# Attention plus a Fourier mix on one core: a unit's maxima split and turned on VectorE instead of by a matmul with the identity

## The chip, the cores and the metric

The kernel runs on one core of one Trainium2 chip. The metric is the device time of one execution in microseconds (us); the time of a kernel is the median of its runs. Before the change it is 1856.32 us over 3 runs (1855.99 to 1856.41).

## The reference

Sequence length 2048, width 640, 32 heads of 20. Two branches are computed from the same `x` and mixed by a gate of each row:

```python
g = _sigmoid((x * gate_w).sum(-1, keepdims=True))
# branch A: softmax attention
scores = jnp.einsum("bhqd,bhkd->bhqk", q, k) * (Dh ** -0.5)
p = _softmax(scores, axis=-1)
o = jnp.einsum("bhqk,bhkd->bhqd", p, v)
a = o.transpose(...).reshape(B, S, D) @ wo
# branch B: real part of a DFT over width and sequence
y = Cr @ (x @ Wd_re.T) - Ci @ (x @ Wd_im.T)
return g * a + (1 - g) * y
```

The weights are scaled so that scores are large: the softmax needs the true maximum of each query's scores. The change concerns how that maximum gets from where it is computed to where it is subtracted.

## The kernel before, in words

Everything is float32, most of it as "float32r" parts: a number is split into a rounded part and a remainder, and products are sums of three part products. Work on TensorE is of six kinds, and the text names each by its source line:

- projections (`qk_tile`, `v_pair`, lines 119 to 121): 128 rows of the array, stationary tile of 128 columns;
- **m** matmuls (line 197): scores of 128 queries (stationary, from `q`) against 512 keys (moving, from `k`), 60 rows of the array, either rows 0 to 59 or rows 64 to 123 (one head of a pair in each half). Only their maximum over the keys is wanted: VectorE reduces each 128x512 result to a 128x1 column of the tile `mx` (line 199);
- **e** matmuls (line 949): the scores again, transposed (keys stationary, queries moving), 62 rows: 60 of `k` and `q` and 2 rows in which `k` is one and `q` holds the negated maximum in two parts, so that the maximum is subtracted in the matmul. ScalarE reads the result through the exponential (line 951);
- **F**, filler matmuls of the Fourier branch and of the output (lines 378, 635, 742): 64 rows each, issued in pairs, one for each half of the array;
- **AV** matmuls (line 556): probabilities times values, in **bursts** (all 128 rows of the array);
- one small matmul by the identity for each unit (line 231), below.

A *unit* is a pair of heads and half the queries: 32 units of 32 steps, a step being two m (or two e) matmuls. The m matmuls run 41 steps (`LEAD`) ahead of the e matmuls. The order of TensorE's work is written by hand in `ORDERS`: each cycle is a string of e, m, F and at the end B, the burst. There are three stages. From about 250 to 596 us a cycle has 8 e, 8 m, filler of the hidden DFT and a burst of 16 AV instructions. From about 600 to 1639 us a cycle has 12 e, 12 m, 48 filler matmuls of the sequence DFT and a burst of 24 AV instructions. From then to the end the filler is the output projection. Before 250 us the projections run, with the first m steps in between (`now[0] < 0` in the code).

The e and m results rotate through five PSUM banks (`bank()`), so a matmul can start only when the result five places earlier has been read.

**The turn of a unit.** At the unit's last m step the maxima of 128 queries x 8 query tiles x 2 heads stand in `mx`, a query in each partition. They are needed as rows: two single partitions of `q` for each head, 1024 queries long. Before, this takes: `max_nm` (line 213), one VectorE reduction over the four key blocks with a negation, into `nm` (128x16); `max_chain` (line 231), a TensorE matmul of `nm` with the identity into a PSUM bank of the rotation (16x128; the float32 matmul is two instructions); `split` on VectorE (lines 115 and 116), a copy to the rounded part `m1` and a subtraction to the remainder `m2`, both 16x128 and both reading that bank; and four DMAs on SP's queue (lines 239 and 240), each moving 8 partitions of 128 into one row of `q`, issued two steps later (`at_step`).

Where the turn lies is set in `burst` and in the loop at the end: if the unit's last m came before the cycle's ninth m of the second stage, `max_nm` is issued there and `max_chain` stands before the last AV step of the burst (call this *inside*); otherwise `max_nm` stands ahead of the burst and `max_chain` behind it (*behind*). In the second stage a cycle has 6 steps and a unit 32, so of three units in a row one is of the second sort. A turn comes once in about 5.3 cycles there, and once in 8 cycles of the first stage.

`dft_step` also gives VectorE an addition (line 655) at every second burst of the second stage, through `run_extras` in `burst`; `unit_end` gives it a reciprocal (line 577) for each unit.

`load_stack(0)` (line 436) loads the first `kst` and `qst` tiles by 12 DMAs from POOL's queue at about 60 us. Behind it on POOL stand the memsets of the `v` tiles (line 352), which ScalarE's evictions of the V projection (line 356) wait for.

Of the kernel before, what the change touches and what calls it, by code (L numbers as in the profile page):

```python
# [19 lines left out]
P = 128  # L20
# [9 lines left out]
KROWS = 3 * DH  # L30
NU = 2 * NP
# [41 lines left out]
def f32(ap):  # L73
    return ap.bitcast(F32)
# [3 lines left out]
def mix_kernel(ctx: ExitStack, tc: tile.TileContext, xa, wqk, wb, cdft, wo, out):  # L78
    nc = tc.nc
    pe, act, dve, pool, sp = nc.tensor, nc.scalar, nc.vector, nc.gpsimd, nc.sync  # L80
# [6 lines left out]
    small = pools(name="small", bufs=1)  # L87
# [13 lines left out]
    ident = const.tile([P, P], F32, name="ident")  # L101
# [2 lines left out]
    qst = [const.tile([P, S], R, name=f"qst{i}") for i in range(2)]  # L104
    for t in kst:
        pool.memset(f32(t), 1.0)
    logit = const.tile([P, NS], F32, name="logit")
    gate = const.tile([P, NS], F32, name="gate")
    ngate = const.tile([P, NS], F32, name="ngate")

    def split(dst1, dst2, src, e1, e2):
        if e1 is act:
            act.activation(dst1, src, AF.Copy)  # L113
        else:
            e1.tensor_copy(dst1, src)
        e2.tensor_tensor(dst2, src, f32(dst1), op=ALU.subtract)  # L116
# [11 lines left out]
    def bank():  # L128
        places.rotate(-1)
        return place_tile(places[-1])  # L130
# [49 lines left out]
    mx, nms, ends = {}, {}, []  # L180
    now, later = [-1], {}

    def at_step(i, fn):
# [3 lines left out]
    def s_mm(i, h):  # L187
        n, s = divmod(i, 32)
        if n >= NU:
            return lambda: None  # L190
        qt, kc = divmod(s, 4)
        q, k = q_unit(n), k_stack(n)
        if n not in mx:
            mx[n] = small.tile([P, 2, 8, 4], F32, name="mx", bufs=2)
        ps = bank()
        b = 64 * h
        pe.matmul(ps, q[b : b + KROWS, qt * P : (qt + 1) * P],  # L197
                  k[b : b + KROWS, kc * 512 : (kc + 1) * 512], start=True, stop=True)
        return lambda: dve.tensor_reduce(mx[n][:, h, qt, kc : kc + 1], ps, axis=AX.X, op=ALU.max)  # L199

    def s_end(i):
        n, s = divmod(i, 32)
        if n < NU and s == 31:
            if now[0] < 0:
                max_nm(n)
            else:
                ends.append(n)
        if s == 1 and 0 < n <= NU and now[0] < 0:
            max_chain(n - 1)

    def max_nm(n):
        nms[n] = small.tile([P, 16], F32, name="nm", bufs=2)
        dve.tensor_reduce(nms[n], mx.pop(n).rearrange("p h q c -> p (h q) c"), axis=AX.X, op=ALU.max, negate=True)

    def s_step(i):
        for fn in [s_mm(i, h) for h in range(2)]:
# [10 lines left out]

    def max_chain(n):
        q = q_unit(n)
        pt = bank()[:16, :P]  # L230
        pe.matmul(pt, nms.pop(n), ident, start=True, stop=True)  # L231
        m1 = small.tile([16, P], R, name="m1")
        m2 = small.tile([16, P], R, name="m2")
        split(m1, m2, pt, dve, dve)

        def rows():
            for h in range(2):
                b = 64 * h + KROWS
                sp.dma_start(f32(q[b : b + 1, :]), f32(m1[8 * h : 8 * h + 8, :]))
                sp.dma_start(f32(q[b + 1 : b + 2, :]), f32(m2[8 * h : 8 * h + 8, :]))  # L240

        if now[0] < 0:
            rows()
        else:
            at_step(now[0] + 2, rows)
# [187 lines left out]
    fin()  # L433
    flush()
    for args in load_stack(0):
        pool.dma_start(*args)
    fin = load_wqk(1)
    for s in range(12, 16, 2):
        v_pair(0, s)
# [2 lines left out]
    order = [1, ND + 1, 2, ND + 2, 3, ND + 3, 4, ND + 4]  # L442
# [16 lines left out]
    for n, c in enumerate(order):  # L459
        for t in range(4):  # L460
            m = 4 * n + t
# [362 lines left out]
    start = 4 * HID  # L824
# [152 lines left out]
    for c in range(len(goals)):  # L977
        k, base, i = phase(c)
        order, *heads_ = ORDERS[k]
        first = dict(zip("em", heads_))  # L980
        for x, kind in enumerate(order):
            if kind == "F":
                fill(c)
            elif kind == "B":
                burst(c)
            else:
                if k == 1 and kind == "m" and order[:x].count("m") == 8:
                    for n in ends:
                        max_nm(n)
                score(kind)  # L990
            if k == 1 and x == len(order) // 2:
                run_loads(c - HID)
# [114 lines left out]
```

## Time and profile before

| What | Value |
|---|---|
| Median of 3 runs | 1856.32 us |
| Span of the profiled execution, first to last instruction | 1852.1 us |
| What lies around the span (median less span) | 4.2 us |
| TensorE (PE) busy | 1844.1 us, 100% of the span |
| VectorE (DVE) busy | 1379.7 us, 74% |
| ScalarE (ACT) busy | 1357.0 us, 73% |
| GpSimd (POOL) busy | 1003.6 us, 54% |
| Granted TensorE clock, mean | 0.999 |

The profile is of one execution. In the timeline a row is a start in us from the start of the span, a duration, the engine (PE is the matmul, PEld the load of its stationary tile, SPq the DMA queue of SyncE), the source line, the operation, output and input, and a count where equal instructions have been merged; in square brackets stands the idle time before it and what ended that. In the groups by line, the columns behind the count are busy us, mean ns of one, and idle us before. A matmul's shape is written rows*columns of the array, then moving tile.

### The profile page before, as it was taken

To read this page: it belongs to the slowest core of one execution; us is meant where nothing else is said; L and a number is where in the kernel's file an instruction comes from. 1 tells how busy PE (TensorE), PEld (TensorE's weight loads), DVE (VectorE), ACT (ScalarE), POOL (GpSimd) and SP (SyncE) were. 2 spreads that over 40 slices of the span, in tenths; PEclk is the share of its full clock that TensorE was granted. 3 is DMA by queue.
4 is the path that set the end of the run, shared out by engine and by line. 5 is a ranking of instruction groups with operands and counts; after the bars stand their busy time and mean duration, and the time that the engine had idled before them with its cause. 6 is when DMAs were issued, how large, how long until landed. Compare 5 with 4: busy or idle time off the path is not lost.

```text
span 1852.1 us, 44874 instructions
## 1 busy us (share of the span) xinstructions
PE 1844.1 (100%) x17638; PEld 1365.3 (74%) x17638; DVE 1379.7 (74%) x2309; ACT 1357.0 (73%) x2645; POOL 1003.6 (54%) x832
## 2 busy tenths in 40 slices
PE   9999999999999999999999999999999999999998
PEld 8988777676776777777777777777777777776666
DVE  3044458888787888888888888888888888888853
ACT  4222258878787888888788888888888877778885
POOL 4334432121136676344677788655668767645644
PEclk9999999999999999999999999999999999999999
DMA  7744341222135574636566586646475856531233
GB/s 236 173 136 157 136 126 56 79 64 67 58 92 149 200 215 148 157 118 194 177 201 227 159 261 197 192 140 183 130 235 189 246 163 206 178 91 55 82 99 109
DMA packets 178771, 281.61 MB, mean 152 GB/s; under 512 B 44811, under 2 KB 113547, under 8 KB 178559
## 3 DMA queue, kind: packets, MB, share of 16 engines
q1 hardware_dynamic: 177599, 276.77, 49.1%
q0 software_dynamic: 960, 1.97, 0.6%
q8 instruction: 138, 2.26, 0.5%
q14 instruction: 74, 0.61, 0.1%
HBM read 214.61 MB, written 63.52 MB: 150 GB/s over the span
## 4 chain that ended last, share of the span: by engine, by line
PE 99%; DMA 0%; DVE 0%; ACT 0%; POOL 0%; SPq 0%; issue 0%; POOLq 0%; ACTq 0%
PE ps L556 25%; PE yp L635 19%; PE ps L949 17%; PE ps L197 14%; PE yp L378 7%; PE ps L119 4%; PE ps L120 4%; PE ps L121 4%; PE yp L742 3%; DMA p<-in_xa 0%; PE ps L231 0%; DVE mx L199 0%; PE ps L1041 0%; POOL x L1010 0%; PE yp L1062 0%
## 5 line engine op out<-in xcount | busy, mean ns | idle before, releaser
L199 DVE TENSOR_REDUCE mx<-ps 128x1 f32<-128x512 f32 x2048 | 1280.6, 684 | 305.8 <-PE ps L197 235.8
L951 ACT ACTIVATE p<-ps 128x512 f32<-128x512 f32 x2048 | 1055.1, 612 | 282.4 <-PE ps L197 159.3
L949 PE MATMUL ps<-qst,kst 62*128 62x512 f32 x1920 | 727.7, 406 | 0.2
L197 PE MATMUL ps<-kst,qst 60*128 60x512 f32 x1920 | 664.3, 409 | 0.0
L635 PE MATMUL yp<-x,part 64*128 64x320 f32 x5376 | 628.1, 306 | 0.0
L635 PEld LDWEIGHTS yp<-x,part 64*128 64x128 f32 x5376 | 601.7, 186 | 5.2
L556 PE MATMUL ps<-p,v 128*21 128x512 f32 (+1 forms) x4096 | 482.0, 595 | 0.0
L116 POOL TENSOR_TENSOR part<-raw,part 128x1024 fp32r<-128x1024 f32 (+1 forms) x128 | 287.4, 2246 | 338.3 <-ACT part L113 322.4
L949 PEld LDWEIGHTS ps<-qst,kst 62*128 62x128 f32 x1920 | 341.3, 185 | 155.5 <-DVE mx L199 86.4
L197 PEld LDWEIGHTS ps<-kst,qst 60*128 60x128 f32 x1920 | 323.3, 184 | 11.8 <-issue 4.2
L556 PEld LDWEIGHTS ps<-p,v 128*21 128x21 f32 (+1 forms) x4096 | 104.8, 101 | 236.1 <-issue 228.6
L378 PE MATMUL yp<-wb,x 64*128 64x320 f32 x1920 | 223.9, 307 | 0.0
L378 PEld LDWEIGHTS yp<-wb,x 64*128 64x128 f32 x1920 | 209.8, 186 | 6.5 <-ACT raw L388 0.2
L389 POOL TENSOR_TENSOR raw<-raw 128x320 f32<-128x320 f32 x64 | 55.6, 869 | 267.0 <-ACT raw L388 210.0
L515 POOL TENSOR_TENSOR raw<-raw,raw 128x1024 f32<-128x1024 f32 x77 | 187.4, 2434 | 1.5 <-DMA raw<-in_cdft 1.5
L113 ACT ACTIVATE part<-raw 128x1024 fp32r<-128x1024 f32 (+2 forms) x121 | 123.4, 1020 | 2.0 <-DMA raw<-in_wqk 1.9
L742 PE MATMUL yp<-x,part 64*128 64x320 f32 x768 | 102.2, 308 | 0.0
L116 POOL TENSOR_TENSOR x<-araw,x 128x320 fp32r<-128x320 f32 x112 | 97.4, 877 | 1.3
L338 ACT ACTIVATE p<-ps 128x512 f32<-128x512 f32 x40 | 23.7, 597 | 100.1 <-PE ps L121 97.1
L742 PEld LDWEIGHTS yp<-x,part 64*128 64x128 f32 x768 | 92.0, 186 | 1.3
L119 PE MATMUL ps<-x,part 128*128 128x512 f32 x200 | 79.9, 400 | 0.5 <-ACT x L113 0.3
L120 PE MATMUL ps<-x,part 128*128 128x512 f32 x200 | 78.6, 393 | 0.4 <-DVE x L116 0.4
(101 smaller groups left out, 1364.2 us busy)
## 6 DMA issues: line engine op xcount, KB each, us to landing
raw<-in_cdft SPq DMA_DIRECT2D x192, 512.0 KB
araw<-a_scr SPq DMA_DIRECT2D x192, 160.0 KB
qk_scr<-p SPq DMA_DIRECT2D x40, 512.0 KB
kst<-qk_scr SPq DMA_DIRECT2D x84, 160.0 KB
qst<-qk_scr SPq DMA_DIRECT2D x84, 160.0 KB
yt<-y_scr SPq DMA_DIRECT2D x80, 160.0 KB
a_scr<-raw SPq DMA_DIRECT2D x64, 160.0 KB
y_scr<-yt SPq DMA_DIRECT2D x64, 160.0 KB
```

The lines of the kernel that those rows point to most:

```text
L116: e2.tensor_tensor(dst2, src, f32(dst1), op=ALU.subtract)
L119: pe.matmul(ps, st1, mv1, start=first, stop=False)
L120: pe.matmul(ps, st1, mv2, start=False, stop=False)
L197: pe.matmul(ps, q[b : b + KROWS, qt * P : (qt + 1) * P], k[b : b + KROWS, kc * 512 : (kc + 1) * 512], start=True, stop=True)
L199: return lambda: dve.tensor_reduce(mx[n][:, h, qt, kc : kc + 1], ps, axis=AX.X, op=ALU.max)
L378: pe.matmul(yp[h][:, :HE], x[r, xz, d, cs], w[r, wz, d, :HE], start=d == 0 and z == 0, stop=d == ND - 1 and z == 2)
L515: pool.tensor_tensor(raws[0], raws[0], raws[1], op=ALU.add if PRODUCTS[n][0][1][0] > 0 else ALU.subtract)
L556: pe.matmul(t[32 * j : 32 * j + m, :], v[:, r : r + m], pp[qc][:, h, :], start=kt == 0, stop=kt == NS - 1)
L635: pe.matmul(yp[h][:, :HE], c[r, cz, cs], a[r, az], start=s == 0 and z == 0, stop=s == NS - 1 and z == 2)
L742: pe.matmul(yp[h][:, :HE], o[oz][r], wos[d, hf][r, wz], start=d == 0 and z == 0, stop=end)
L949: pe.matmul(pt, k[b : b + KROWS + 2, kt * P : (kt + 1) * P], q[b : b + KROWS + 2, qc * 512 : (qc + 1) * 512], start=True, stop=True)
L951: act.activation(pts[n, kt, qc][:, h], pt, AF.Exp, scale=float(DH) ** -0.5)
```

## The change

The line numbers of before and after differ by one or two; the diff has the code.

- `mx` is reduced over the key blocks three times in `max_chain`: the maximum (plane 1), the negated maximum written as float32r, which is its rounded part (plane 0), and the negated sum of the two, which is the remainder (plane 2). All three go to a tile `turn` (128 x 8 x 32 of float32), which is cleared once at the start of the program.
- `dve.transpose` turns each 32x32 block of `turn` into `turned` (128 x 256).
- The identity matmul, its PSUM bank, `nm`, `m1`, `m2` and the split are gone, as is the call of `max_nm` in mid-cycle. All four VectorE instructions now stand in one piece ahead of the burst's AV matmuls, behind `run_extras`.
- So that a turned row comes out in query order, the stationary tile of an m matmul is no longer 128 neighbouring queries but every eighth one: its columns lie 8 float32 (32 bytes) apart in `q`. The moving tile is unchanged.
- Each of the four row DMAs now reads 4 partitions of 256 elements.
- `load_stack(0)` goes to SP's queue, and the scratch space of software DMA is set to 4096.

```diff
+    turn = [small.tile([P, 8, 32], F32, name="turn"), small.tile([P, 256], F32, name="turned")]
+    pool.memset(turn[0], 0.0)
...
-        pe.matmul(ps, q[b : b + KROWS, qt * P : (qt + 1) * P],
+        pe.matmul(ps, q[b : b + KROWS, :].rearrange("r (c t) -> r t c", t=8)[:, qt],
                   k[b : b + KROWS, kc * 512 : (kc + 1) * 512], start=True, stop=True)
...
-    def max_nm(n):
-        nms[n] = small.tile([P, 16], F32, name="nm", bufs=2)
-        dve.tensor_reduce(nms[n], mx.pop(n).rearrange("p h q c -> p (h q) c"), axis=AX.X, op=ALU.max, negate=True)
...
     def max_chain(n):
         q = q_unit(n)
-        pt = bank()[:16, :P]
-        pe.matmul(pt, nms.pop(n), ident, start=True, stop=True)
-        m1 = small.tile([16, P], R, name="m1")
-        m2 = small.tile([16, P], R, name="m2")
-        split(m1, m2, pt, dve, dve)
+        top = mx.pop(n)
+        m = turn[0].rearrange("p t (h z c) -> p z h t c", h=2, z=4)[:, :, :, :, 0]
+        dve.tensor_reduce(m[:, 1], top, axis=AX.X, op=ALU.max)
+        dve.tensor_reduce(m[:, 0].bitcast(R), top, axis=AX.X, op=ALU.max, negate=True)
...
+            dve.tensor_reduce(m[:, 2].bitcast(R), m[:, :2].rearrange("p z h t -> p h t z"), axis=AX.X, op=ALU.add, negate=True)
+        dve.transpose(turn[1].rearrange("p (c t) -> p t c", t=8), turn[0])
...
-                sp.dma_start(f32(q[b : b + 1, :]), f32(m1[8 * h : 8 * h + 8, :]))
-                sp.dma_start(f32(q[b + 1 : b + 2, :]), f32(m2[8 * h : 8 * h + 8, :]))
+                for z in range(2):
+                    b = 64 * h + KROWS + z
+                    src = turn[1].rearrange("(b j) c -> j b c", b=4)[16 * h + 8 * z]
+                    sp.dma_start(f32(q[b : b + 1, :]), src)
...
     for args in load_stack(0):
-        pool.dma_start(*args)
+        sp.dma_start(*args)
...
     def burst(c):
-        ready = any(n in nms for n in ends)
-        for n in ends:
-            if n not in nms:
-                max_nm(n)
         k, _, i = phase(c)
         steps = 6 if k == 1 else 4
         run_extras(steps - 2)
+        while ends:
+            max_chain(ends.pop(0))
...
-            if ready and kt == (i + steps) // 2 - 1:
-                max_chain(ends.pop(0))
             av_step(now[0], kt // NS, kt % NS, kt % NS == 0 and kt > i // 2)
-        while ends:
-            max_chain(ends.pop(0))
...
-                if k == 1 and kind == "m" and order[:x].count("m") == 8:
-                    for n in ends:
-                        max_nm(n)
```

Where the instructions stand. First TensorE at a turn of the second stage that lies behind the burst (the one at 684 us in the trace), before; `ps` is a bank of the rotation, the 556 row the burst:

```order
L197 MATMUL ps_9535<-kst_86,qst_88 128x512
L197 MATMUL ps_9538<-kst_86,qst_88 128x512
L556 MATMUL ps_9058<-p,v 21x512 x12
L231 MATMUL ps_9563<-ident,nm 16x128
L949 MATMUL ps_9570<-qst_88,kst_86 128x512
L197 MATMUL ps_9574<-kst_87,qst_89 128x512
```

The same place after (m is now line 199, e 948, AV 555):

```order
L199 MATMUL ps_9502<-kst_86,qst_88 128x512
L199 MATMUL ps_9505<-kst_86,qst_88 128x512
L555 MATMUL ps_9025<-p,v 21x512 x12
L948 MATMUL ps_9533<-qst_88,kst_86 128x512
L199 MATMUL ps_9537<-kst_87,qst_89 128x512
```

The identity matmul and its bank have gone; nothing else on TensorE has moved. Now VectorE at a turn inside a burst (the one at 637 us), before; `mx` rows are reductions of m results, 655 the Fourier addition:

```order
L213 TENSOR_REDUCE nm<-mx 128x16
L199 TENSOR_REDUCE mx<-ps_8694 128x1
L199 TENSOR_REDUCE mx<-ps_8697 128x1
L199 TENSOR_REDUCE mx<-ps_8703 128x1
L199 TENSOR_REDUCE mx<-ps_8706 128x1
L655 TENSOR_TENSOR m<-yp_8427,m 128x320
L115 CAST m_8726<-ps_8724 16x128
L116 TENSOR_TENSOR m_8727<-ps_8724,m_8726 16x128
L199 TENSOR_REDUCE mx<-ps_8739 128x1
```

The same place after:

```order
L201 TENSOR_REDUCE mx<-ps_8672 128x1
L201 TENSOR_REDUCE mx<-ps_8675 128x1
L654 TENSOR_TENSOR m<-yp_8398,m 128x320
L228 TENSOR_REDUCE turn<-mx 128x2x8
L229 TENSOR_REDUCE turn<-mx 128x2x8
L231 TENSOR_REDUCE turn<-turn 128x2x8
L232 STREAM_TRANSPOSE turned<-turn 128x8x32
L201 TENSOR_REDUCE mx<-ps_8706 128x1
```

Three instructions in two places have become four in one place, behind the four reductions that are due at the burst, and behind the addition where there is one. Last, SP's queue at about 60 us, after (before, the two rows of line 435 are not there and the row of `raw<-in_wqk` follows that of `v_scr`):

```order
L329 DMA qk_scr<-p 128x2x512 x2
L329 DMA v_scr<-v 128x8x84 x2
L435 DMA kst_86<-qk_scr 20x4x512 x6
L435 DMA qst_88<-qk_scr 20x4x512 x6
L300 DMA raw<-in_wqk 128x640
L329 DMA v_scr<-v 128x8x84 x4
```

Twelve loads now stand ahead of a weight load and four stores.

More of the change, by code (lines that the diff above doesn't have):

```diff
@@ L178, in q_unit @@
         return third["q"] if p == 14 else qst[place(p)][:, u * (S // 2) : (u + 1) * (S // 2)]
-    mx, nms, ends = {}, {}, []
+    mx, ends = {}, []
     now, later = [-1], {}
@@ L204, in s_end @@
             if now[0] < 0:
-                max_nm(n)
+                max_chain(n)
             else:
                 ends.append(n)
-        if s == 1 and 0 < n <= NU and now[0] < 0:
-            max_chain(n - 1)
-    def max_nm(n):
-        nms[n] = small.tile([P, 16], F32, name="nm", bufs=2)
-        dve.tensor_reduce(nms[n], mx.pop(n).rearrange("p h q c -> p (h q) c"), axis=AX.X, op=ALU.max, negate=True)
     def s_step(i):
@@ L986, in mix_kernel @@
             else:
-                if k == 1 and kind == "m" and order[:x].count("m") == 8:
-                    for n in ends:
-                        max_nm(n)
                 score(kind)
@@ L1095 @@
     arrays = {k: c(a) for k, a in arrays.items()}
-    nc = bacc.Bacc("TRN2", target_bir_lowering=False, num_devices=1)
+    nc = bacc.Bacc("TRN2", target_bir_lowering=False, num_devices=1, dynamic_dma_scratch_size=4096)
     args = {
```

2 lines of the change are left out of this document (1 added, 1 removed).

## The prediction

> **What bounds the kernel now.** I read the page first (busy shares, the chain that ended last), then the groups of TensorE and VectorE by shape, then the timeline of TensorE around turns and around bursts without one.
>
> ```profile
> span 1852.1 us, 44874 instructions
> PE 1844.1 (100%) x17638; PEld 1365.3 (74%) x17638; DVE 1379.7 (74%) x2309; ACT 1357.0 (73%) x2645; POOL 1003.6 (54%) x832
> ...
> PE 99%; DMA 0%; DVE 0%; ACT 0%; POOL 0%; SPq 0%; issue 0%; POOLq 0%; ACTq 0%
> ...
> L199 DVE TENSOR_REDUCE mx<-ps 128x1 f32<-128x512 f32 x2048 | 1280.6, 684 | 305.8 <-PE ps L197 235.8
> ```
>
> The end is set by TensorE: it is never idle and 99% of the chain is its own work. VectorE has a quarter of the span free on the whole, 93% of its work being the reductions of m results. So two questions decide: how much of TensorE's time the turn costs, and whether the new form costs any in another place.
>
> The rhythm of the bursts answers the first. These are AV bursts (line 556) of the second and the first stage, and the identity matmuls (231) among them:
>
> ```profile
> 634.78 1.92 PE L556 MATMUL ps<-p,v 128*21 128x512 f32 x16
> 644.29 2.77 PE L556 MATMUL ps<-p,v 128*21 128x512 f32 x24
> ...
> 681.49 2.77 PE L556 MATMUL ps<-p,v 128*21 128x512 f32 x24
> 684.08 0.38 PE L231 MATMUL ps<-ident,nm 128*16 128x128 f32 x2
> 691.26 2.77 PE L556 MATMUL ps<-p,v 128*21 128x512 f32 x24
> ...
> 700.57 2.77 PE L556 MATMUL ps<-p,v 128*21 128x512 f32 x24
> 709.87 1.49 PE L556 MATMUL ps<-p,v 128*21 128x512 f32 x12
> ...
> 257.33 1.92 PE L556 MATMUL ps<-p,v 128*32 128x512 f32 x16
> ...
> 263.49 1.92 PE L556 MATMUL ps<-p,v 128*21 128x512 f32 x16
> ...
> 288.16 1.91 PE L556 MATMUL ps<-p,v 128*21 128x512 f32 x16
> ...
> 294.52 1.91 PE L556 MATMUL ps<-p,v 128*21 128x512 f32 x16
> ```
>
> Without a turn, 691.26 to 700.57 is a cycle of 9.31 us, and the next, to 709.87, is 9.30. With a turn inside the burst, 634.78 to 644.29 is 9.51: 0.20 more. With a turn behind it, 681.49 to 691.26 is 9.77: 0.46 more. In the first stage a cycle is 6.16 (257.33 to 263.49), with a turn 6.36 (288.16 to 294.52): 0.20 more. A cycle this regular, on an engine without idle time, gets shorter by what is taken out of it.
>
> **Removed from TensorE.** Where the 0.20 and the 0.46 come from shows which of it goes:
>
> ```profile
> L231 PE MATMUL ps<-ident,nm 128*16 128x128 f32 x64 | 12.2, 273 | 0.4 <-DVE nm L213 0.4
> ...
> PEld ps L949 <- DVE m L116: 9.1, 14, 0.8
> ...
> 217.31 0.39 PE L231 MATMUL ps<-ident,nm 128*16 128x128 f32 x2 [0.35 <-DVE nm L213]
> ```
>
> The pair at 684.08 takes 0.38 with 0.27 for one, so the second starts 0.11 after the first, and two fill 0.21 of TensorE: that is the 0.20. The rest of the 0.46 is a wait: the third e behind the burst comes to the identity's bank in the rotation of five and finds that the split has not read it. The row of waits puts such e matmuls down to line 116. VectorE at that place, and the e in question:
>
> ```profile
> 681.14 2.48 DVE L199 TENSOR_REDUCE mx<-ps 128x1 f32<-128x512 f32 x4 [0.30 <-PE ps L197]
> 683.66 0.22 DVE L213 TENSOR_REDUCE nm<-mx 128x16 f32<-128x64 f32 x1
> 684.50 0.28 DVE L115 CAST m<-ps 16x128 fp32r<-16x128 f32 x1 [0.62 <-PE ps L231]
> 684.81 0.28 DVE L116 TENSOR_TENSOR m<-ps,m 16x128 fp32r<-16x128 f32 x1
> 685.02 1.27 DVE L199 TENSOR_REDUCE mx<-ps 128x1 f32<-128x512 f32 x2
> 685.14 0.18 PEld L949 LDWEIGHTS ps<-qst,kst 62*128 62x128 f32 x1 [0.45 <-DVE m L116]
> ```
>
> The split ends at 685.09 and the load of the e starts at 685.14. With the bank out of the rotation both parts go. The turns are 7 in the first stage, 21 in the second (7 behind the burst, 14 inside), 3 in the last, and the first one at 217.31, in the projections, where TensorE waited 0.35 for the maxima. Sum: 24 x 0.20 = 4.8 (7 + 14 + 3), 7 x 0.46 = 3.2, and 0.35 + 0.20 = 0.6 at the first: **8.6 us off TensorE**, which is the path that sets the end.
>
> **Added on VectorE.** Rows for the price:
>
> ```profile
> L655 DVE TENSOR_TENSOR m<-yp,m 128x320 f32<-128x320 f32 x56 | 26.9, 481 | 0.0
> ...
> L1063 DVE TENSOR_TENSOR o<-o,yp 128x256 f32<-128x256 f32 x2 | 0.8, 421 | 0.4 <-PE yp L1062 0.3
> L1057 DVE COPY rb<-lc 128x512 f32<-128x512 f32 x1 | 0.4, 427 | 0.0
> ...
> 703.84 1.91 DVE L199 TENSOR_REDUCE mx<-ps 128x1 f32<-128x512 f32 x3 [1.14 <-PE ps L197]
> ```
>
> Two of the new reductions read the same 64 elements as line 213: 0.22 each. The third reads 32: at most 0.22, say 0.19. The trace has no transpose. It moves 256 elements per partition: the addition of 256 took 0.42 and the copy of 512 took 0.43, so about 0.42, nearest to the first; the copy's rate on 256 would give less, 0.3; and if the scattered writes (32 bytes apart) cost a second pass, about 0.7. The piece is then 0.22 + 0.22 + 0.19 + 0.42 = **1.05 us**, between 0.9 and 1.35. Removed are 0.22 + 0.28 + 0.28 = 0.78 and the 0.62 for which VectorE stood and waited for the identity. Over the run VectorE's load grows by 32 x 0.27 = 9 us in 1380, which alone costs nothing.
>
> What counts is when it is done, because the reductions that free banks are queued behind it. At the burst at 681.49 the four due reductions end at 683.62; the piece would end at 684.67. When the first result behind a burst is due, the last row shows: after the burst at 700.57 VectorE stood idle for 1.14 and began again at 703.84, which is 3.27 after the burst's start. From 681.49 that gives 684.76. So where nothing else stands ahead, 25 of 32 times by the order, the piece is covered by the burst. In the other 7 the addition of line 655 (0.48, about 0.40 net of overlap) comes first, and VectorE is free at about 685.05: 0.3 late. No row shows how long a bank stands read before it is needed again, so I let half of the 0.3 reach TensorE: 7 x 0.15 = **1.0 us back**, between 0 and 7 x 0.5 = 3.5.
>
> **The strided stationary tile** is the change's open price. The load of an m takes part in the path only if it outlasts the matmul before it in the same half of the array:
>
> ```profile
> 1835.04 1.00 PEld L1055 LDWEIGHTS yp<-ident,o 128*128 128x128 f32 x8
> ...
> 215.76 0.89 PE L378 MATMUL yp<-wb,x 64*128 64x320 f32 x9
> ...
> 703.61 0.62 PE L949 MATMUL ps<-qst,kst 62*128 62x512 f32 x2
> ...
> L197 PEld LDWEIGHTS ps<-kst,qst 60*128 60x128 f32 x1920 | 323.3, 184 | 11.8 <-issue 4.2 <-DVE mx L199 0.3 <-ACT p L951 0.3
> ```
>
> Line 1055 has moving tiles of 4 columns, so its loads follow each other as fast as they can: (1.00 - 0.19) / 7 = 0.116 us for 128 columns. Filler matmuls in one half follow each other in 2 x (0.89 - 0.31) / 8 = 0.146, and the two e at 703.61 in 0.62 - 0.39 = 0.23. So a load hides with 0.03 to spare behind a filler and with 0.11 behind an e or m. All loads now are of neighbouring columns; the trace has none with a stride. I take the stride at nothing: a load passes a column in 0.116 / 128 = 0.9 ns, while the moving side passes one in 0.146 / 320 = 0.46 ns, so a load asks only half the rate of columns that these reads give elsewhere, and it has 0.03 of cover. The other end is a rival below.
>
> **The queues.** Each row DMA still reads into one row of 4 KB, four for each turn; by the `LEAD` of 41 steps a unit's first e comes 9 steps (some 14 us) behind its last m, and no wait of TensorE for DMA stands in the chain. Cost 0. The loads moved to SP:
>
> ```profile
> 63.56 0.53 SPq L301 DMA_DIRECT2D raw<-in_wqk  x1
> ...
> 68.66 0.58 POOL L436 DMA_DIRECT2D qst<-qk_scr  x1 [0.67 <-DMA kst<-qk_scr]
> ...
> 69.94 0.77 ACT L356 ACTIVATE v<-ps 128x320 f32<-128x320 f32 x2 [5.37 <-POOL v L352]
> ...
> 75.93 0.74 ACT L113 ACTIVATE part<-raw 128x640 fp32r<-128x640 f32 x1 [1.32 <-DMA raw<-in_wqk]
> 80.66 0.45 ACT L356 ACTIVATE v<-ps 128x320 f32<-128x320 f32 x1 [3.99 <-POOL v L352]
> ```
>
> POOL's memset of `v` no longer waits until 69.24 for its own issues, so ScalarE evicts earlier than 69.94. Against that the weight load of line 301 moves behind 12 issues of about 0.5, some 6 us, and ScalarE stands at line 113 for it with evictions queued behind. TensorE has no wait here now, so there is nothing to gain; the banks cover a few us of lateness. I take 0, with +5 as the bad end.
>
> **Sum.** 1856.3 - 8.6 + 1.0 = 1848.7 us; the profiled span would go from 1852.1 to about 1844.5, with the same 4.2 around it. Without the extremes of the open prices the forecast's own range is 1846.5 to 1851.
>
> **The rivals.** *VectorE's piece becomes the wait.* If the piece takes 1.35 us or more, or the banks have less slack than I think, it is late by 0.3 at 14 of the turns of the second stage and by 0.6 at the 7 with an addition: 14 x 0.2 + 7 x 0.5 = 6.3 back, and the time is about 1854; with a late start on top, 1857. For it speaks that reductions run with little idle time there; against it that VectorE's idle time is given back at every burst and that at the turn of 684 us it began again only at 685.02 and the cycle lost no more than the wait for the bank.
>
> *The strided load is slower (the other side).* If a column in a line of its own takes a second access, a load takes 0.23, and behind a filler an m is late by 0.23 - 0.146, some 0.08. By `ORDERS` 6 of 12 m of a second-stage cycle and 6 of 8 of the first follow a filler in their half: 112 x 6 + 56 x 6 + about 160 = 1170 of 2048. At 0.08 that is 94 us if each holds up both halves, half if the halves' delays fall together: 47. Less the gain, 1895 to 1942, say 1910. It decides as soon as a load passes 0.146 + 0.007 (8 us over 1170). For it speaks that the reads are spread over eight times the bytes; against it the slow rate of loads. [...]
>
> *It doesn't do what it says.* The order shows the identity matmuls gone from TensorE, so this is out.
>
> **How the numbers follow.** The forecast has 0.65, VectorE's piece 0.15, the strided load 0.20. The prediction is the likeliest case's 1848.7. The range leaves out the strided load and takes in the rest: 1846 to 1857. A measurement of this kernel can tell about 0.2%, 3.7 us, from no change, so faster is under 1852.6: the forecast whole and a little of the second case, 0.67; the same is the rest of the second case, 0.12; slower is the strided load and a late start, 0.21.
>
> **What would show it.** Right: bursts 9.30 us apart with and without a turn, no line 231 on TensorE, and a load of an m still at 184 ns. Wrong in the price of VectorE: turns where cycles are still 9.5 or more, with e or m waiting for a reduction. Wrong in the stride: loads of m longer than those of e (185 ns), and cycles without a turn longer than 9.31. Wrong at the start: TensorE waits between 60 and 90 us.

## The result, and the profile after

The kernel after takes 1928.37 us (median of 4 runs, 1926.93 to 1928.84), beside 1856.37 (1855.99 to 1857.54) for the one before: a ratio of 1.0389, 95% interval 1.0376 to 1.0403. It is slower by 72 us, where 7.6 less were forecast.

The head of the page after, with the chain's shares by engine:

```profile
span 1926.4 us, 44734 instructions
PE 1913.2 (99%) x17574; PEld 1462.7 (76%) x17574; DVE 1414.5 (73%) x2341; ACT 1383.6 (72%) x2645; POOL 995.9 (52%) x821
...
PE 98%; DMA 1%; DVE 0%; SPq 0%; POOL 0%; ACT 0%; issue 0%; POOLq 0%; DVEq 0%; ACTq 0%
```

TensorE still sets the end, with 64 instructions fewer and 69 us more of busy time. The loads of stationary tiles (PEld) have grown by 97. Waiting is little of it (TensorE's listed waits were 2.5 in all before and are 7.0 now); TensorE's own work has become longer. The groups by shape say which. The load and matmul of m (199) and of e (948):

```profile
L199 PEld LDWEIGHTS ps<-kst,qst 60*128 60x128 f32 x1920 | 512.0, 315 | 6.3 <-issue 4.2 <-DVE mx L201 1.6 <-ACT p L950 0.3
L948 PEld LDWEIGHTS ps<-qst,kst 62*128 62x128 f32 x1920 | 356.9, 191 | 158.3 <-DVE mx L201 85.5 <-DVE m L654 45.8 <-DVE turn L231 14.4
...
L199 PE MATMUL ps<-kst,qst 60*128 60x512 f32 x1920 | 774.1, 488 | 1.0 <-DVE mx L201 1.0
L948 PE MATMUL ps<-qst,kst 62*128 62x512 f32 x1920 | 713.1, 404 | 0.0
```

A load of an m takes 315 ns instead of 184, 131 more; a load of an e, whose tile is not strided, 191. Now the rhythm: bursts (line 555) in the second and in the first stage, each with the one transpose (232) that falls among them:

```profile
702.23 2.77 PE L555 MATMUL ps<-p,v 128*21 128x512 f32 x24
711.93 2.77 PE L555 MATMUL ps<-p,v 128*21 128x512 f32 x24
721.67 0.63 PE L555 MATMUL ps<-p,v 128*21 128x512 f32 x4
...
714.68 0.70 DVE L232 STREAM_TRANSPOSE turned<-turn 128x256 f32<-128x256 f32 x1
...
291.40 1.91 PE L555 MATMUL ps<-p,v 128*21 128x512 f32 x16
297.93 1.91 PE L555 MATMUL ps<-p,v 128*21 128x512 f32 x16
304.46 1.92 PE L555 MATMUL ps<-p,v 128*21 128x512 f32 x16
...
299.43 0.67 DVE L232 STREAM_TRANSPOSE turned<-turn 128x256 f32<-128x256 f32 x1
```

The cycle with the turn, 711.93 to 721.67, is 9.74, the one before it, without, 9.70; over the stage cycles without a turn are 9.72 in the median. In the first stage both are 6.53. The turn's 0.20 and 0.46 are gone, but every cycle is longer: 9.72 against 9.30 and 6.53 against 6.16. That is most of the balance: 56 cycles of the first stage by 0.37 less its 7 turns make 19.3 (measured from the first burst on, 349.5 became 368.9), 111 of the second by 0.42 less 21 turns make 40.6 (1039.0 became 1079.8). The last stage, to its last burst, takes 5.3 more, the rest behind that burst 0.9 more (19.72 became 20.65, all of it behind TensorE's last matmul), and the time to the first burst grew by 7.9, from 257.33 to 265.25. Together that is the 74.3 between the two spans. The medians differ by 72.0, since before's profiled execution was shorter than its median: in every run whose span is listed the time is 1.7 to 1.8 above the span, which puts it at about 1853.9. So the 4.2 given above as lying around the span compares two different executions.

TensorE's waits after, the longest four, and the place of the second:

```profile
PE ps L121 <- ACT x L115: 2.9, 1, 2.9
PE ps L121 <- ACT logit L359: 1.6, 1, 1.6
PE ps L415 <- POOL ident masks.py:199: 1.3, 1, 1.3
PE ps L199 <- DVE mx L201: 1.0, 1, 1.0
```

```profile
69.41 5.13 SPq L435 DMA_DIRECT2D qst<-qk_scr  x6
75.38 0.37 SPq L300 DMA_DIRECT2D raw<-in_wqk  x1
...
83.43 0.74 ACT L115 ACTIVATE part<-raw 128x640 fp32r<-128x640 f32 x1 [9.20 <-DMA raw<-in_wqk]
85.91 0.45 ACT L355 ACTIVATE v<-ps 128x320 f32<-128x320 f32 x1 [1.75 <-POOL v L351]
...
86.47 0.41 PE L121 MATMUL ps<-wb,x 128*128 128x322 f32 x1 [1.61 <-ACT logit L359]
```

The weight load is issued at 75.38 behind the moved loads, before it was at 63.56; ScalarE stands 9.20 for it and 1.75 more for the memset, with its evictions queued behind, and TensorE waits 1.61. The 2.9 at 9 us comes at a place where the change adds only the clearing of `turn`; the kernel before itself shows 0.3 there in one execution and 2.2 in another (e12), so most of it is put down to chance. VectorE's piece at last, by instruction:

```profile
L232 DVE STREAM_TRANSPOSE turned<-turn 128x256 f32<-128x256 f32 x32 | 22.0, 688 | 1.1
L228 DVE TENSOR_REDUCE turn<-mx 128x16 f32<-128x64 f32 x32 | 6.8, 212 | 0.3
```

### The profile page after: what moved, and what is told of

It is laid out like the page before. It is cut to its first block, busy times and chain, and to the rows that moved or that the text cites. A ratio compares the mean times of both kernels' runs of the same rounds, so it can differ in the third digit from the quotient of the medians.

```text
span 1926.4 us, 44734 instructions
## 1 busy us (share of the span) xinstructions
PE 1913.2 (99%) x17574; PEld 1462.7 (76%) x17574; DVE 1414.5 (73%) x2341; ACT 1383.6 (72%) x2645; POOL 995.9 (52%) x821
## 4 chain that ended last, share of the span: by engine, by line
PE 98%; DMA 1%; DVE 0%; SPq 0%; POOL 0%; ACT 0%; issue 0%; POOLq 0%; DVEq 0%; ACTq 0%
PE ps L555 24%; PE yp L634 20%; PE ps L199 17%; PE ps L948 17%; PE yp L377 7%; PE ps L121 3%; PE ps L123 3%; PE ps L122 3%; PE yp L741 3%; DMA v_scr<-v 1%; DMA kst<-qk_scr 0%; DMA p<-in_xa 0%; DVE mx L201 0%; SPq L435 0%; PE ps L1031 0%; POOL x L1000 0%
## 5 line engine op out<-in xcount | busy, mean ns | idle before, releaser
L201 DVE TENSOR_REDUCE mx<-ps 128x1 f32<-128x512 f32 x2048 | 1300.8, 684 | 351.6 <-PE ps L199 327.0
L950 ACT ACTIVATE p<-ps 128x512 f32<-128x512 f32 x2048 | 1082.1, 600 | 321.6 <-PE ps L948 207.2
L199 PE MATMUL ps<-kst,qst 60*128 60x512 f32 x1920 | 774.1, 488 | 1.0 <-DVE mx L201 1.0
L948 PE MATMUL ps<-qst,kst 62*128 62x512 f32 x1920 | 713.1, 404 | 0.0
L634 PE MATMUL yp<-x,part 64*128 64x320 f32 x5376 | 649.2, 305 | 0.0
L634 PEld LDWEIGHTS yp<-x,part 64*128 64x128 f32 x5376 | 618.2, 187 | 1.7
L199 PEld LDWEIGHTS ps<-kst,qst 60*128 60x128 f32 x1920 | 512.0, 315 | 6.3 <-issue 4.2
L948 PEld LDWEIGHTS ps<-qst,kst 62*128 62x128 f32 x1920 | 356.9, 191 | 158.3 <-DVE mx L201 85.5
L377 PE MATMUL yp<-wb,x 64*128 64x320 f32 x1920 | 243.6, 307 | 0.0
L377 PEld LDWEIGHTS yp<-wb,x 64*128 64x128 f32 x1920 | 234.9, 189 | 1.0 <-ACT raw L387 0.4
L741 PE MATMUL yp<-x,part 64*128 64x320 f32 x768 | 106.8, 307 | 0.0
L337 ACT ACTIVATE p<-ps 128x512 f32<-128x512 f32 x40 | 23.8, 597 | 102.9 <-PE ps L123 99.8
L741 PEld LDWEIGHTS yp<-x,part 64*128 64x128 f32 x768 | 96.6, 188 | 0.7
```

The costliest lines, as they stand in the source:

```text
L199: pe.matmul(ps, q[b : b + KROWS, :].rearrange("r (c t) -> r t c", t=8)[:, qt], k[b : b + KROWS, kc * 512 : (kc + 1) * 512], start=True, st ...
L377: pe.matmul(yp[h][:, :HE], x[r, xz, d, cs], w[r, wz, d, :HE], start=d == 0 and z == 0, stop=d == ND - 1 and z == 2)
L634: pe.matmul(yp[h][:, :HE], c[r, cz, cs], a[r, az], start=s == 0 and z == 0, stop=s == NS - 1 and z == 2)
L741: pe.matmul(yp[h][:, :HE], o[oz][r], wos[d, hf][r, wz], start=d == 0 and z == 0, stop=end)
L948: pe.matmul(pt, k[b : b + KROWS + 2, kt * P : (kt + 1) * P], q[b : b + KROWS + 2, qc * 512 : (qc + 1) * 512], start=True, stop=True)
L950: act.activation(pts[n, kt, qc][:, h], pt, AF.Exp, scale=float(DH) ** -0.5)
```

## The experiments

Ratios are each against runs of the kernel before on the same chip, whose medians were 1854.0 to 1856.4. In e3, e6 and e7 the exponential is taken of zero times the score, so that every probability is one; the instructions and their number stay the same. "Neighbours" is the kernel after with m's stationary tile of 128 neighbouring queries again; the turned blocks then go to rows in pieces of 32 queries, by eight row DMAs instead of four.

### The stride alone, and the stride taken back

**e3**: the kernel before with the one line of the stride.

```diff
-        pe.matmul(ps, q[b : b + KROWS, qt * P : (qt + 1) * P],
+        pe.matmul(ps, q[b : b + KROWS, :].rearrange("r (c t) -> r t c", t=8)[:, qt],
```

> The kernel before with nothing changed but the stationary tile of an m, every eighth query; the exponential's scale is zero, since the maxima then stand in another order. Theory (the stride is the whole loss and the turn a gain of its own): the time after plus the turn's 8.6 less the 1.6 at 86 us, that is 1932 to 1938. Rival (the turn's pieces share in the loss): 1900 to 1926.

It took 1930.93 (ratio 1.0405, 1.0391 to 1.0418). Its load of an m:

```profile
L197 PEld LDWEIGHTS ps<-kst,qst 60*128 60x128 f32 x1920 | 513.3, 316 | 4.9 <-issue 4.2 <-ACT p L951 0.3 <-DVE mx L199 0.3
```

The time is 1 under the range of its theory and above its rival's. So the stride costs 75 us by itself (0.0405 of 1856), and the turn shows up again on top of the longer cycles: 9.74 without, 9.94 and 10.09 with one, 6.52 and 6.73 in the first stage. Against e3, which has the stride and the old turn, the three stages of the kernel after are shorter by 0.3, 6.6 and 0.6 (369.2, 1086.4 and 192.3 became 368.9, 1079.8 and 191.8): under the stride the turn gains 7.4.

**e1**: neighbours, the rest as after. **e2**: e1 with the first loads on GpSimd's queue again, and with the scratch space of software DMA as before.

```diff
-        pe.matmul(ps, q[b : b + KROWS, :].rearrange("r (c t) -> r t c", t=8)[:, qt],
+        pe.matmul(ps, q[b : b + KROWS, :].rearrange("r (g c t) -> r g t c", c=P, t=1)[:, qt // 1, qt % 1],
...
-        dve.transpose(turn[1].rearrange("p (c t) -> p t c", t=8), turn[0])
+        dve.transpose(turn[1].rearrange("p (g c t) -> p g t c", c=32, t=1), turn[0].rearrange("p (g t) r -> p g t r", t=1))
...
+                for j in range(4):
+                    b = 64 * h + KROWS
+                    dst = q[b : b + 2, :].rearrange("z (g j x) -> j z g x", j=4, x=32 * 1)[j]
```

> The kernel after, with the stationary tile of an m taken again from 128 neighbouring queries; the turned rows are put in order by eight row DMAs of two rows each in place of four. Theory (the strided load is the whole loss, the turn's gain is there beneath it): loads of an m back at 184 ns, second-stage cycles 9.30 us with and without a turn, time 1849 to 1853 (1856.4 less 8.6, plus 1.6 to 4.5 that the start lost in the kernel after). Rival (the VectorE piece or the row DMAs also cost): cycles with a turn 9.5 or more, time 1855 to 1865. Rival (the loss is elsewhere): time stays above 1900.

> As e1, and the first load of the kst and qst tiles back on POOL's queue, as before the change. Theory (moving the 12 loads to SP costs the wait of TensorE near 86 us): e1 less 1.6 to 4.5 us, that is 1847 to 1849, and no wait of TensorE between 60 and 100 us. Rival (that wait is chance): the same time as e1 within 0.5 us.

e1 took 1882.8 (1.0152, 1.0134 to 1.0170), e2 1878.95 (1.0132, 1.0112 to 1.0151), where 1847 to 1853 had been expected of the two; e1's rivals (1855 to 1865, over 1900) missed it too. The load of an m in e2:

```profile
L199 PEld LDWEIGHTS ps<-kst,qst 60*128 60x128 f32 x1920 | 323.8, 186 | 15.1 <-issue 4.2 <-ACT p L950 2.1 <-DVE mx L201 1.9
```

Cycles without a turn are at 9.32 and 6.16, and of the 21 turns of the second stage 7 lie in cycles of 9.31 or 9.32: the stride's cost is gone, and so is the turn's own. Seven more, those with an addition, have up to 9.45, and the remaining seven 11.5 to 12.8, for another reason. The transpose takes 446 ns here, with its writes in a row. In e1 TensorE waits 2.2 at 85 us (after: 1.6), in e2 not at all there, so the loads on SP's queue are what that wait came from; the medians differ by 3.9, with intervals that overlap. But both lose elsewhere. The row DMAs of e2, and the e behind them:

```profile
748.88 5.37 SPq L239 DMA_DIRECT2D qst<-turned  x8
...
755.44 0.60 PE L948 MATMUL ps<-qst,kst 62*128 62x512 f32 x1 [1.91 <-DMA qst<-turned]
```

Eight issues take 5.37, where four before took 2.8, and for every third unit the rows come 1.9 late, seven times. What such a wait costs can be more than its length. Busy time by stretch around it; the columns after the length are PE, PEld, DVE, ACT and POOL with counts, then the granted clock and the DMA share:

```profile
735.00:745.00 10.00, 10.00 (x110) 7.54 (x108) 8.72 (x16) 8.41 (x17) 4.14 (x4) 1.00 0.01 1
...
755.00:758.00 3.00, 2.56 (x18) 2.42 (x18) 0.26 (x1) 0.60 (x1) 0.00 (x0) 0.60 0.86 272
758.00:762.00 4.00, 4.00 (x32) 1.10 (x30) 2.62 (x5) 2.29 (x4) 1.89 (x1) 0.87 0.93 271
762.00:766.00 4.00, 4.00 (x49) 3.92 (x46) 3.82 (x6) 4.00 (x10) 0.50 (x1) 1.00 0.75 158
```

Behind the wait the granted clock is 0.60 and then 0.87 until 762. The cycle in which it lies is 12.74 long (bursts at 745.74 and 758.48), 3.4 over 9.32. So a wait of 1.9 cost 3.4 here. It is not always so: behind the waits at 1061 and 1214, 1.9 and 2.0 long, the granted clock stays at 1.00, and those two cycles lost 2.2. The seven cost 22 together by the length of their cycles and of the next, and two waits at the end of the first stage (2.6 and 1.4) about another 10; that is nearly all of the 34 by which e2's profiled execution lies over that of e14 (below), where no e waits for rows.

### How far apart, and on which side

**e4** and **e5** are e2 with columns 8 and 16 bytes apart (`t=2` and `t=4` in the lines above, instead of 1; 32 bytes is `t=8`).

> As e2, with the columns of an m's stationary tile every second query, 8 bytes apart. [...] Rival (any gap between columns costs): loads near 315 ns and 1915 to 1925. Rival (the cost grows with the distance): loads near 200 to 220 ns, hidden behind the filler, and 1848 to 1853.

> As e2, with the columns every fourth query, 16 bytes apart. [...] Rival (the cost grows with the distance): loads near 250 ns, 0.17 without the latency, behind a filler 0.03 late: 1865 to 1885.

e4 took 1878.64 (1.0129, 1.0102 to 1.0155), the same as e2. e5 took 1932.78 (1.0429, 1.0403 to 1.0455), far over the 1865 to 1885 of its rival; like e2 it waits seven times for rows, 1.8 to 2.0 each. Their loads of m, e4 first:

```profile
L199 PEld LDWEIGHTS ps<-kst,qst 60*128 60x128 f32 x1920 | 334.8, 193 | 13.5 <-issue 4.2 <-DVE mx L201 1.8 <-ACT p L950 0.6
```

```profile
L199 PEld LDWEIGHTS ps<-kst,qst 60*128 60x128 f32 x1920 | 498.0, 307 | 6.6 <-issue 4.2 <-DVE mx L201 1.6 <-ACT p L950 0.5
```

Side by side in steps of 4, 8, 16 and 32 bytes: 186, 193, 307, 315 ns. The cost is not one that grows with the distance: from 8 bytes to 16 it is 114 ns, from 4 to 8 it is 7 and from 16 to 32 it is 8. With columns 16 or 32 bytes apart these loads pay, at 8 hardly. What makes the step, no run shows.

**e8**: e9 (below) with the *moving* tile of m taking every fourth key, 16 bytes apart, the stationary one neighbours.

```diff
-                  k[b : b + KROWS, kc * 512 : (kc + 1) * 512], start=True, stop=True)
+                  k[b : b + KROWS, :].rearrange("r (c t) -> r t c", t=4)[:, kc], start=True, stop=True)
```

> As e9, with neighbouring queries in the stationary tile, and the moving tile of an m taken from every fourth key, 16 bytes apart (the maximum over all keys is the same). [...] Rival (only loads suffer): 1848 to 1852.

It took 2067.91 (1.1152, 1.1136 to 1.1169), far over the 1848 to 1852 by which only loads would suffer. The matmul of m, e9 first, then e8:

```profile
L199 PE MATMUL ps<-kst,qst 60*128 60x512 f32 x1920 | 668.4, 412 | 1.2 <-DVE mx L201 1.2
...
L199 PE MATMUL ps<-kst,qst 60*128 60x512 f32 x1920 | 960.6, 630 | 0.3 <-DVE mx L201 0.3
```

It is 218 ns longer, 0.43 ns for each of 512 columns, about as much as a column took (0.46, the 0.146 / 320 of the fillers before). The load's 131 over 128 columns are 1.02 ns each, on top of 0.9. As an estimate from these numbers, both sides fall to about half their rate, each from its own: the load from 0.9 to 1.9 ns a column, the moving tile from 0.46 to 0.89.

### Which m pay

**e9** is e2 with every second row DMA issued by GpSimd; it serves as the base here. **e6** gives the 32-byte stride only to those m whose predecessor in their half of the array is a filler, **e7** only to the others.

```diff
+        t = 8 if before[h] == "F" else 1
+        before[h] = "m"
+        pe.matmul(ps, q[b : b + KROWS, :].rearrange("r (g c t) -> r g t c", c=P, t=t)[:, qt // t, qt % t],
```

(e7 has `!= "F"`.)

> As e9, but an m whose predecessor in its half of the array is a filler takes its stationary columns 32 bytes apart; all others take neighbours. The exponential's scale is zero, since the maxima are then of mixed queries. Theory (a load costs only what it outlasts the matmul before it: some 0.24 against 0.146): nearly the whole loss, cycles near 9.70 in the second stage, 1912 to 1925. Rival (each strided load costs the same wherever it stands): about 57 per cent of the loss, 1885 to 1895.

> The counterpart of e6: 32 bytes apart only where the predecessor in the half is an e, an m or the burst; scale zero as there. Theory (a load of 0.24 behind a 512-column matmul of 0.23 is hidden but for 0.01): cycles 9.30 to 9.36, 1848 to 1857. Rival (each strided load costs the same): about 43 per cent of the loss, 1875 to 1885.

e6 took 1914.64 (1.0328, 1.0312 to 1.0343), 55 over e9, with some 1200 strided loads: 0.046 each, as its theory had it. e7 took 1883.0 (1.0155, 1.0138 to 1.0172), 24 over e9, with some 840. The second was not expected: behind an e or m the load was taken to have the 0.23 of that matmul as cover, and these should have been nearly free. (It lies in the range of e7's rival, by which each strided load costs the same; e6, 20 above its range of that rival, speaks against that reading.) The cycles give the place, 0.15 longer in the second stage and 0.09 in the first. TensorE behind a burst, e9 first, then e7 (there m is line 202, e 954):

```profile
750.55 0.50 PE L948 MATMUL ps<-qst,kst 62*128 62x512 f32 x1
750.55 0.73 PE L199 MATMUL ps<-kst,qst 60*128 60x512 f32 x2
750.89 0.40 PE L948 MATMUL ps<-qst,kst 62*128 62x512 f32 x1
```

```profile
747.78 0.50 PE L954 MATMUL ps<-qst,kst 62*128 62x512 f32 x1
747.79 0.74 PE L202 MATMUL ps<-kst,qst 60*128 60x512 f32 x2
748.25 0.51 PE L954 MATMUL ps<-qst,kst 62*128 62x512 f32 x2
```

The first e and m stand behind the burst together; the second e comes 0.34 after the first in e9 and 0.47 in e7. The loads there start beside the matmuls that need them, after 0.85 without a load (at 750.54 in e9, at 747.78 in e7), and the two of m take 0.29 together in e9 and 0.42 in e7. If these 0.13 go into the path once a cycle, they make 111 x 0.13 = 14 of the 24. That the loads hand the delay on is read from the starts in the trace; no run moved them. The two halves of the experiment sum to 79, close to the 75 of e3.

### Whether the turn's gain stands, with neighbours

**e9**, **e10**, **e11**, **e13** and **e14** try to bring e2's rows in time. e10 takes the turn in the second stage after the cycle's eighth m instead of at the burst. e9 gives half of the row DMAs to GpSimd's queue, e11 to ScalarE's; e13 is e10 and e9 together, e14 is e10 with the half on GpSimd in the first stage only.

```diff
 # e10, e13, e14, in the loop at the end
                 if k == 1 and kind == "m" and order[:x].count("m") == 8:
+                    while ends:
+                        max_chain(ends.pop(0))
 # e9, e13: pool; e11: act; e14: pool where also now[0] < 224
-                    sp.dma_start(f32(dst), ...)
+                    (pool if j % 2 else sp).dma_start(f32(dst), ...)
```

> As e2, with every second one of the eight row DMAs on POOL's queue. Theory (e2 lost its gain to rows that land late: eight issues of 0.62 us in a row, 7 units whose first e waits 1.9 us, and after such a wait the clock too): no wait of e for the rows, cycles 9.30 to 9.33 us with and without a turn, 1846 to 1850. Rival (something else in e2 costs): 1865 or more. Rival (POOL's issues hold up POOL's own work, and that the fillers): no wait for rows, but cycles over 9.35 and 1852 to 1865.

> As e2 (neighbouring queries, eight row DMAs on SP, first load on POOL), but in the second stage the turn of a unit that has ended by the cycle's eighth m is taken there instead of ahead of the burst. Theory (what is left of e2's loss is rows that come late because the turn waits for the burst): no wait of e for rows in the second stage; the piece of 1.0 us on VectorE in mid-cycle holds up TensorE by 0.3 to 0.7 us in 14 cycles; 1848 to 1856. Rival (eight DMAs on SP also delay others): 1860 or more.

> As e2, with every second one of the eight row DMAs on ScalarE's queue. Theory: rows land 2.5 us earlier, no wait of e for rows, cycles 9.30 to 9.33 us; 1846 to 1851 if ScalarE's issues cost it nothing. Rival (ScalarE stands for each issue, 4 of about 0.6 us a unit, and its exponentials with it): cycles with a turn 10 us or more, 1860 to 1880.

> e10 (the unit's maxima turned after the eighth m of the cycle, from neighbouring queries) with every second of the eight row DMAs issued by GpSimd, so that SyncE has four instead of eight of them. Theory (the whole 8.6 us of the turn stand once the rows are there in time, and e10 lost its 8 us in the first stage to SyncE's queue, where the eight row DMAs stood ahead of other transfers): the waits of 3.5 and 1.2 at 557 to 608 go, the first stage is back at about 348, the second stays at 1036 to 1037, and the time is 1847 to 1852. Rival (the waits in the first stage come from GpSimd's or the DMA rings' own lateness, as the 5.2 at 1498 in e9): 1854 to 1860, with one or two waits of over 3 us, at another place.

> e10 (second stage: turn after the eighth m, all eight row DMAs on SyncE) with every second row DMA issued by GpSimd in the first stage and ahead of it alone. Theory (each queue has one stretch that spoils the turn: SyncE the end of the first stage, GpSimd the second stage, where its own splits of 2.4 stand ahead of its issues): the first stage is 348 as in e9 and e13, the second 1036 as in e10, the last 200.7, no wait of TensorE over 3 us behind the start, and the time is 1847 to 1850 beside 1854 to 1856 for the kernel before, ratio 0.996 to 0.998. Rival (the 8 us are paid back in some place whatever the queue): 1854 to 1859, with a wait of over 2 us at a place that none of e9, e10 and e13 shows.

| Kernel | us | Ratio to before (95%) | First stage | Second | What TensorE waited for |
|---|---|---|---|---|---|
| before | 1856.37 | | 349.5 | 1039.0 | |
| e9 | 1859.26 | 1.0023 (1.0013 to 1.0033) | 348.0 | 1044.2 | rows, 5.2 once, at 1498 |
| e10 | 1857.52 | 1.0009 (0.9997 to 1.0020) | 357.2 | 1036.1 | 3.5 at 567, 1.2 at 608 |
| e11 | 1928.5 | 1.0392 (1.0378 to 1.0405) | 363.8 | 1090.7 | ScalarE, 31 times, up to 2.0 |
| e13 | 1873.39 | 1.0097 (1.0081 to 1.0114) | 348.1 | 1060.2 | rows, 6 times, 1.3 to 3.0 |
| e14 | 1852.57 | 0.9986 (0.9977 to 0.9995) | 348.2 | 1035.4 | nothing behind the first turn |

All five took longer than their theories had it: e9 by 9, e10 by 1.5, e11 by 77, e13 by 21 and e14 by 2.6, each from the upper end of its range. Each queue has a stretch that spoils it. In e11 ScalarE issues four DMAs in front of its exponentials (rows of TensorE's waits):

```profile
PE ps L948 <- ACT p L950: 35.1, 22, 2.0
PE ps L199 <- ACT p L950: 13.8, 9, 1.6
```

In e10 SyncE's issues at the end of the first stage are late; a single store of `a_scr`, elsewhere 0.34, takes 1.97, and before the filler at 567 ScalarE waits 4.72 for such a store. That it is this one is not shown:

```profile
551.01 1.97 SPq L890 DMA_DIRECT2D a_scr<-raw  x1
```

The kernels with all eight rows on SyncE and cycles of 6.16 to 6.18 (e1, e2, e4, e10) wait 1.3 to 3.5 at 565 to 569; none of e9, e13 and e14 does, nor e5 with its cycles of 6.50. Why that issue takes so long was not tried. In e13 the rival (1854 to 1860) was wrong too. GpSimd at a turn, and the e that follows:

```profile
737.26 2.37 POOL L118 TENSOR_TENSOR part<-raw,part 128x1024 fp32r<-128x1024 f32 x1 [5.73 <-ACT part L115]
739.57 2.26 POOL L239 DMA_DIRECT2D qst<-turned  x4
...
744.88 0.47 PE L948 MATMUL ps<-qst,kst 62*128 62x512 f32 x1 [1.31 <-DMA qst<-turned]
```

SyncE began its four rows at 736.10; GpSimd was in a split of 2.37 and began at 739.57, and the e came to the rows before they had landed. Of the six such waits of e13, as of e9's one, the view of waits puts most down to another DMA (`y_scr`, `rb`), which an e doesn't read; all are at an e that starts 3.6 to 5.3 after the start of a turn's last issue, so I take them for waits for the rows. e14 avoids both stretches and has the stages that each half promised. Its page and waits:

```profile
PE 1837.2 (99%) x17574; PEld 1360.8 (74%) x17574; DVE 1385.8 (75%) x2341; ACT 1357.1 (73%) x2645; POOL 1022.0 (55%) x865
...
PE ps L415 <- POOL ident masks.py:199: 1.4, 1, 1.4
PE ps L121 <- ACT x L115: 1.3, 1, 1.3
PE ps L199 <- DVE mx L201: 1.2, 1, 1.2
```

It beats the kernel before by 0.14% (0.05 to 0.23), 2.2 us between the medians, with runs from 1849.7 to 1856.1. In its profiled execution, the fastest of the eleven, TensorE is busy 6.9 less than before, and the three stages are shorter by 1.3, 3.6 and 0.4, 5.3 in all, while the rest behind the last burst is 1.2 longer. So a gain of the turn is there without the stride as well; 5.3 is its size in the stages of this one execution. Bursts of e14, the first cycle with a turn and an addition, the second with neither:

```profile
633.53 2.77 PE L555 MATMUL ps<-p,v 128*21 128x512 f32 x24
643.00 2.77 PE L555 MATMUL ps<-p,v 128*21 128x512 f32 x24
652.34 2.77 PE L555 MATMUL ps<-p,v 128*21 128x512 f32 x24
```

The seven cycles of this kind take 9.35 to 9.73, 1.05 in sum over the median of 9.318; the other 14 turns of the stage lie in cycles of 9.30 to 9.33. In e9, at each of the same seven turns, a load of an e some 4.2 behind the burst's start waits 0.06 to 0.16 for a reduction on VectorE.

**e12** is the kernel before once more, unchanged.

> The kernel before once more, for its profile: how much TensorE waits in its first 15 us, where the profile before has 0.33 at 7.9 us and the kernels since 0.8 to 2.9. Theory (chance of the first loads): a wait anywhere from 0.3 to 3 us. Rival (something in the change delays the start): 0.3 again.

1856.14, with a wait of 2.21 at 9.6 us: a wait of about that length there, as in e1, e7, e9 and the kernel after (2.3 to 2.9), doesn't need the change.

## Why the prediction was wrong

The step that failed is the one that says "I take the stride at nothing: a load passes a column in 0.116 / 128 = 0.9 ns, while the moving side passes one in 0.146 / 320 = 0.46 ns, so a load asks only half the rate of columns that these reads give elsewhere, and it has 0.03 of cover". Both rates were measured on neighbouring columns, and the moving side's says nothing of what a strided read gives: e8 shows it at half its rate as well (0.46 became 0.89 ns a column), and the load went to 1.9 (0.247 / 128). The 0.03 of cover then met 0.13 of extra length. What happened is the rival that had 0.20, and its decisive point, a load over 0.153, was passed by far.

- **The rival's price.** It had 0.23 for the back-to-back load, which is 0.116 doubled; 0.116 + 0.131 is 0.247. That a second access is what takes the time was the author's estimate: no run shows such an access, only the 131 ns. Behind fillers e6 shows 0.046 each, near its lower end of 0.04 for delays of the two halves that fall together. It had counted nothing for other m, and e7 shows 24 there. So 1928 lies inside its 1895 to 1942 and 18 above its 1910.
- **The turn off TensorE, 8.6.** Right in kind, and in the kernel after nearly in size: cycles with and without a turn differ by 0.04 at most, as forecast, and against e3 the stages gain 7.4 where 8.0 stood for them. Without the stride it is less. e14 gains 5.3: its cycles are 9.318 in the median, where those of before without a turn were 9.30 to 9.31, and 111 times that little is 1 to 2; the seven turns with an addition take another 1.05. Why the other cycles are that little longer was not tried. And the first turn, at which 0.6 was to be gained, costs: an m waits 1.0 there for VectorE, where the identity had waited 0.35.
- **VectorE's piece, 1.05.** From the start of the first reduction to the end of the transpose it is 1.33 in the kernel after (714.05 to 715.38). The reductions are 0.21 each, near the 0.22, 0.22 and 0.19 (the third reads the two planes of `turn`, not `mx`). The transpose is 0.69, the end given for scattered writes; with its writes in a row (e2) it is 0.45, near the 0.42. The 1.0 that was to come back from the seven turns with an addition does not show in the kernel after, where their cycles are 9.73 and 9.74 like others; that the longer cycle gives the time is likely, but was not tried. With neighbours and a piece of about 1.1 it is there, 1.05 in e14 and 0.8 in e9, and in e9 by the wait of an e that was forecast. The rival's 6.3 is out.
- **The loads on SP, 0 with a bad end of 5.** 1.6 in the kernel after, 2.2 in e1, nothing in e2. The banks did not cover the lateness whole. The mechanism is the one named (ScalarE stands for the weight load, evictions queue behind it), and the memset adds 1.75 (before it held the same eviction 3.99): it waits for stores that now stand behind the loads.
- **The row DMAs, 0.** Right for the four rows of the kernel after: no e waits for them. The margin is thin, though, since eight issues in a row are already 1.9 late for every third unit.

Put together: 1856.4 before, 75.2 for the stride (e3), 1.6 for the late weight load, 0.45 more at the first turn (1.0 less 0.35 and 0.20) and 0.9 behind the last burst, less the 7.4 of the stages, make 1927.2, and 1928.37 was measured. That is as close as the terms allow, each of which is known to about 1 us. The range failed with the step; it had left out the strided load, on the strength of a comparison between rates that did not bear on a stride.

## What to carry to other kernels

When a layout change makes an operand strided, don't price it by the rate of an unstrided read, nor in proportion to the distance; measure it at that step. Here a load with float32 columns 4 or 8 bytes apart took 186 and 193 ns, with 16 or 32 it took 307 and 315, and a matmul with its moving columns 16 bytes apart took 630 instead of 412 (8 bytes were not tried there). Where TensorE never idles, count for each load what stands ahead of it in its half (behind a filler a strided load cost 0.046 us in e6), and look at the place behind a burst, where the second e came 0.13 us later in e7. And a transfer that moves to another queue takes on what already stands there: with the same row DMAs, SyncE (a wait of 3.5 in e10), ScalarE (31 waits of up to 2.0 in e11) and GpSimd (6 of 1.3 to 3.0 in e13) each lost time at a different place.

## What was not expected of the hardware

- A wait of TensorE of 1.9 can be followed by a granted clock of 0.60 over 3 us and 0.87 over 4 more, and its cycle lost 3.4 (e2, at 755); the clock dropped behind five of e2's seven such waits, and behind two it stayed at 1.00 and the cycle lost 2.2. Kernels with several such waits show a mean clock of 0.991 (e11), 0.992 (e2) and 0.995 (e13), against 0.999 before; e5, with seven waits of 1.8 to 2.0, shows 0.999.
- VectorE's transpose of 128x256 float32 takes 446 ns with its writes in a row (e2), 447 with them 8 bytes apart (e4), 646 at 16 (e5) and 688 at 32 (after): a step between 8 and 16 bytes, where TensorE's loads have theirs (193 and 307), here on the writing side.
